# Recurrence with gated MLP on one core: level six and the state's products moved up behind the products into y

## The chip, the cores and the metric

The kernel runs on one core of a Trainium2 chip. The metric is device time in microseconds of one launch. The median before the change is 585.6 us over three runs (585.32 to 585.61). Engines are named as the profile names them: PE is TensorE's matmul, PEld its weight load, DVE is VectorE, ACT is ScalarE, POOL is GpSimd, and SP issues most of the transfers.

## The reference

All arrays are float32. The first half is a linear recurrence with a decay per channel (batch 4, 8 heads, 768 tokens, head size 48). The second half is a two-layer MLP on the 3072 tokens (384 to 2048 to 384).

```python
for t in range(S):
    kt, vt, rt, wt = k[:, :, t], v[:, :, t], r[:, :, t], w[:, :, t]
    cur = einsum('bhd,bhe->bhde', u[None] * kt, vt)
    y[:, :, t] = einsum('bhd,bhde->bhe', rt, state + cur)
    state = wt[:, :, :, None] * state + einsum('bhd,bhe->bhde', kt, vt)
x = y.transpose(0, 2, 1, 3).reshape(B * S, H * D)
h = x @ w_in
out = (h * erf(softplus(h))) @ w_out
```

## The kernel before

The work runs in 12 steps. A step takes 128 tokens of two batch items: 16 heads, as 8 columns n times two halves e of the partitions. Step s works on item pair s mod 2, so the state of a pair is handed on two steps later.

Inside a step the 128 tokens fall into two blocks of 64 (`HC`). What tokens of a block add to each other is found in levels: level L multiplies the right half of each block of 2^L tokens with the left half of it. `scale(s, L)` (L328) multiplies the decays of the halves into r and k in place, so level L must be through TensorE before its scaling, and its scaling before level L+1. `level_products` (L552) makes the small products, 64x32 or 32x32 on a quarter of the array, and `take_level` puts them into `own`: on VectorE with a mask for level five (L562), on ScalarE for level six (L569). The steps 5 to 11 are called late; there, levels one to four are made by VectorE and GpSimd instead, on rows of 16 tokens each.

A late step (`attend_late`) does this, and the order in the code is the order on each engine, since the schedule is manual:

- `from_own(before, ..., 1)` and `fence` (L593): half of the products of the step before into the accumulator `y`. Then level five, its scaling and its take.
- `from_own(before, ..., 0)` and `through_state` (L610): the other half, and the products of the state with r into `y`. ScalarE copies the result to `xT`, the input of the MLP.
- level six and `spread_blocks(s + 1, pp)` (L672), two small products that bring the decays `over_blocks` of the next step onto 64 partitions; ScalarE copies them to `few`, and two transfers (`g_rows`, `spread`) carry them back, spread over 128 partitions.
- `kT *= spread` (L718) on VectorE, `state_part` (L659) on TensorE: k times v for both blocks. `middle` (L736) is the state between the two blocks, `S_next` (L743) that after them. `faded` (L713, L739) is the state times its decay, on GpSimd.
- `prepare(s + 1)`, a generator called `following`: its pieces are GpSimd's products of decays (L402, `tot_sb`, and `over_blocks`), the terms for distances 1 to 15 between tokens (`term`, L463 and L467; 0 to 4 on VectorE, beginning at L470, 5 to 15 on GpSimd in room that the first sums set free), their sums (L453), and the way over `by_blocks` and `by_tokens` into the next `own` (L514). `kT` of the next step takes the same kind of way over `k_blocks`.

Between these stands MLP work, laid out by letters in `USUAL` and `LATE`, one string for each of the stages front, near, 0, 1, 2, 3, 4. `H` is a piece of the hidden layer of step s-1: 12 large products (L1027, counted as passes: 6 products show as 12) into a tile `m`, copied to `h` by ScalarE (L1036). `P` is a piece of the projection of step s-3: 8 products (`project_fast`, L1142) into one of two `m` tiles, with ScalarE copies (L1148, L1153, L1156) and VectorE adds (L1162 reads the first, L1167 the second). `s`, `e` and `m` are softplus (L983), erf (L987, into `y` or the second small PSUM tile) and multiply (L992) of a chunk of h. `S1` to `S4` are blends of h (L1119, L1121, L1125, L1123), `k..` copies for them (L1100), and `F` is the next piece of `following`. `w` is one of four differences of weights, made once (L1194).

`ps_m` has two buffers: the H pieces and the projection take turns in them. `ps_p` has two tiles, pp0 and pp1, one buffer each: a new tile of a name waits until the old one is read.

Of the kernel before, what the change touches and what calls it, by code (L numbers as in the profile page):

```python
# [11 lines left out]
FP32 = mybir.dt.float32  # L12
# [5 lines left out]
P = 128  # L18
# [43 lines left out]
def kernel(  # L62
# [50 lines left out]
    over_blocks = const.tile([P, C // NEAR, JP], FP32, name="over_blocks")  # L113
# [240 lines left out]
    def prepare(s):  # L354
# [61 lines left out]
        if s == DIRECT:  # L416
            yield
        else:
            half = view(tots[NEAR_LOG + 1], 1, [[2, NC], [C >> NEAR_LOG + 1, JP]])
            quarter, last = (  # L420
                view(tots[NEAR_LOG], n, [[4, NC], [C >> NEAR_LOG, JP]]) for n in (1, 3)
            )
            to = over_blocks[:].rearrange("p (h b) n -> p b h n", h=NC)
            nc.gpsimd.tensor_mul(to[:, 0], quarter, half)
            nc.gpsimd.tensor_copy(out=to[:, 1], in_=half)
            nc.gpsimd.tensor_copy(out=to[:, 2], in_=last)
            yield
# [239 lines left out]
    def spread_blocks(s, pp):  # L667


        n = D // 2  # L670
        for e in range(NE):
            nc.tensor.matmul(  # L672
                pp[:EP, e, 0:2, HC // 2 : HC // 2 + n],
                lhsT=over_blocks[rows(e)].rearrange("p b n -> p (b n)"),
                rhs=ident[rows(e), rows(e)], start=True, stop=True,
            )
        few = att.tile([EP, NE * 2, n], FP32, name="few", bufs=1)
        nc.scalar.copy(
            few[:].rearrange("p (e i) d -> p e i d", e=NE),
            pp[:EP, :, 0:2, HC // 2 : HC // 2 + n],  # L680
        )
        g_rows = dram.tile([C // NEAR, JP * NE * D], FP32, name="g_rows")
        nc.sync.dma_start(
            out=g_rows[:].rearrange("b (n d) -> (b n) d", n=JP),
            in_=few[:].rearrange("p i d -> p (i d)"),
        )
        spread[s] = att.tile([P, JP, NE, D], FP32, name="spread", bufs=1)
        nc.sync.dma_start(
            out=spread[s][:].rearrange("p n e d -> p (n e d)"),
            in_=g_rows[:, None, :].to_broadcast([C // NEAR, NEAR, JP * NE * D]),  # L690
        )

    def attend_late(s, run):
# [10 lines left out]
        take_level(own, pp, LOG - 1)  # L704
        run("front", None)
        if before:
            from_own(before, ready[before][0], 0)
            through_state(before, xTs[before])
            if s + 1 < n_steps:
                load_step(s + 1)  # L710
        following = prepare(s + 1) if s + 1 < n_steps else iter(())
        next(following, None)
        nc.gpsimd.tensor_mul(faded[0][:], S[:], ends[:, :, 0:1].to_broadcast([P, JP, D]))  # L713
        next(following, None)
        run("near", None)
        next(following, None)
        kT = kTs[s]
        nc.vector.tensor_mul(  # L718
            kT[:].rearrange("p (e n) d -> p n e d", e=NE),
            kT[:].rearrange("p (e n) d -> p n e d", e=NE), spread[s][:],  # L720
        )
        run(0, following)

        pp = products([P, NE, JP, HC], 0)
        level_products(pp, RK, LOG)
        if s + 1 < n_steps:
            spread_blocks(s + 1, pp)
        take_level(own, pp, LOG)
        scale(s, LOG)
        run(1, following)  # L730
        ps = products([P, NC, JP, HC], 0)
        ps = [[ps[:, h]] * NE for h in range(NC)]
        state_part(s, kT, ps)
        run(2, following)
        for e in range(NE):
            nc.vector.tensor_add(middle[rows(e)], faded[0][rows(e)], ps[0][e][rows(e), :, :D])  # L736
        run(3, following)
# [6 lines left out]
        run(4, following)  # L744
# [575 lines left out]
    def in_order(s, k):  # L1320
# [3 lines left out]
        for what in order[k]:  # L1324
# [15 lines left out]
            "s P", "m w", "ey P m s P P ep P", "m P P", "", "", ""  # L1340
# [72 lines left out]
    with tc.manual_schedule(  # L1413
# [77 lines left out]
        run_late(s - 1, "S Q w w w")  # L1491
# [105 lines left out]
```

## Time and profile before

| what | value |
|---|---|
| median of three runs | 585.6 us |
| the profiled execution | 586.88 us |
| its span, first to last instruction | 585.1 us |
| granted TensorE clock | 0.999 |
| PE busy | 576.4 us (99%) |
| DVE busy | 454.7 us (78%) |
| ACT busy | 355.6 us (61%) |
| POOL busy | 274.1 us (47%) |
| late steps, start of level five | 196.14, 241.46, 286.21, 330.71, 375.21, 419.71, 464.20 us |

A line of a timeline gives the start in the span, the duration, the engine, the line of the code, the operation, the tile written and the tiles read, the shapes and how many instructions were merged. In square brackets stands how long the engine was idle before, and what ended that. TensorE products in float32 show as two passes each, so 32 products count as 64. Consecutive products overlap, so the time a group takes is read from the starts, not from the durations.

### The profile page before, as it was taken

To read this page: it belongs to the slowest core of one execution; us is meant where nothing else is said; L and a number is where in the kernel's file an instruction comes from. 1 tells how busy PE (TensorE), PEld (TensorE's weight loads), DVE (VectorE), ACT (ScalarE), POOL (GpSimd) and SP (SyncE) were. 2 spreads that over 40 slices of the span, in tenths; PEclk is the share of its full clock that TensorE was granted. 3 is DMA by queue.
4 is the path that set the end of the run, shared out by engine and by line. 5 is a ranking of instruction groups with operands and counts; after the bars stand their busy time and mean duration, and the time that the engine had idled before them with its cause. 6 is when DMAs were issued, how large, how long until landed. Compare 5 with 4: busy or idle time off the path is not lost.

```text
span 585.1 us, 16663 instructions
## 1 busy us (share of the span) xinstructions
PE 576.4 (99%) x7240; PEld 495.1 (85%) x7240; DVE 454.7 (78%) x558; ACT 355.6 (61%) x478; POOL 274.1 (47%) x313
## 2 busy tenths in 40 slices
PE   8899999999999999999999999999999999999997
PEld 6588887688668758998898898898898899988997
DVE  6776886999996899799799799799799637256630
ACT  3658877644544598756766666665765771387700
POOL 4557391702398469659459459449549200000000
PEclk9999999999999999999999999999999999999999
DMA  8587571440433414334334334334331301000000
GB/s 269 177 273 281 201 235 44 183 154 10 145 95 116 117 55 156 63 116 165 74 111 169 74 108 172 75 108 136 74 108 55 74 8 36 2 0 2 28 27 29
DMA packets 54082, 63.25 MB, mean 108 GB/s; under 512 B 35160, under 2 KB 40568, under 8 KB 52984
## 3 DMA queue, kind: packets, MB, share of 16 engines
q1 hardware_dynamic: 53624, 61.98, 33.4%
q8 instruction: 57, 0.93, 0.6%
q10 hardware_dynamic: 384, 0.20, 0.1%
q14 instruction: 17, 0.14, 0.1%
HBM read 52.39 MB, written 8.69 MB: 104 GB/s over the span
## 4 chain that ended last, share of the span: by engine, by line
PE 95%; DVE 3%; issue 1%; ACT 0%; POOL 0%; DVEq 0%; POOLq 0%
PE m L1027 36%; PE m L1142 28%; PE m L1059 8%; PE pp L552 6%; PE pp L1230 4%; PE y L1230 2%; PE y L584 2%; PE pp L659 2%; PE y L610 2%; PE m L862 1%; PE pp L871 1%; PE pp L938 1%; DVE in L328 1%; DVE words L467 1%; PE pp L1142 0%
## 5 line engine op out<-in xcount | busy, mean ns | idle before, releaser
L1027 PE MATMUL m<-xT,w_in_sb 128*128 128x256 f32 x960 | 215.3, 382 | 0.1
L1027 PEld LDWEIGHTS m<-xT,w_in_sb 128*128 128x128 f32 x960 | 179.9, 190 | 26.2 <-issue 1.0
L328 DVE TENSOR_TENSOR in<-in,tot_sb 128x1024 f32<-128x1024 f32 (+1 forms) x55 | 75.3, 1369 | 16.5 <-PE pp L552 13.2
L463 POOL TENSOR_TENSOR rk<-words 128x528 f32<-128x528 f32 (+3 forms) x28 | 42.5, 1517 | 91.2 <-DVE sums L453 80.7
L1036 ACT COPY h<-m 128x512 f32<-128x512 f32 x80 | 46.4, 579 | 57.6 <-PE m L1027 57.5
L467 POOL TENSOR_TENSOR words<-words,rest 128x528 f32<-128x528 f32 (+10 forms) x77 | 78.1, 1015 | 6.0
L1059 PE MATMUL m<-w_out_sb,h 128*128 128x384 f32 x192 | 64.3, 491 | 0.0
L1059 PEld LDWEIGHTS m<-w_out_sb,h 128*128 128x128 f32 x192 | 35.7, 190 | 23.5
L1142 PE MATMUL m<-mixed,h 128*128 128x192 f32 x256 | 45.6, 331 | 0.0
L1142 PE MATMUL m<-w_out_sb,h 128*128 128x192 f32 x256 | 44.8, 329 | 0.0
L552 PEld LDWEIGHTS pp<-in 48*64 48x64 f32 (+1 forms) x2368 | 33.4, 126 | 12.0 <-issue 6.2
L1142 PEld LDWEIGHTS m<-mixed,h 128*128 128x128 f32 x256 | 41.4, 190 | 0.9
L1142 PEld LDWEIGHTS m<-w_out_sb,h 128*128 128x128 f32 x256 | 41.6, 190 | 0.3
L1142 PE MATMUL m<-w_out_sb,room 128*128 128x192 f32 x240 | 41.5, 326 | 0.0
L983 ACT ACT_TABLE_LOAD x30 | 38.5, 1283 | 2.7 <-issue 2.2
L987 ACT ACT_TABLE_LOAD x30 | 38.5, 1283 | 1.5 <-DVE room L1125 1.1
L1142 PEld LDWEIGHTS m<-w_out_sb,room 128*128 128x128 f32 x240 | 39.4, 190 | 0.0
L402 POOL TENSOR_TENSOR tot_sb<-tot_sb 128x256 f32<-128x256 f32 (+4 forms) x50 | 36.2, 724 | 3.8
L552 PE MATMUL pp<-in 48*64 48x32 f32 (+1 forms) x2368 | 37.3, 212 | 0.6 <-DVE in L328 0.5
L463 POOL TENSOR_TENSOR words<-words 128x336 f32<-128x336 f32 (+6 forms) x49 | 35.3, 720 | 3.8
L453 DVE TENSOR_REDUCE sums<-rk 128x14 f32<-128x672 f32 (+9 forms) x54 | 34.7, 701 | 0.0
L453 DVE TENSOR_REDUCE sums<-words 128x6 f32<-128x288 f32 (+8 forms) x66 | 26.9, 464 | 3.9 <-POOL words L463 3.6
(198 smaller groups left out, 951.5 us busy)
## 6 DMA issues: line engine op xcount, KB each, us to landing
in<-in_rkw SPq DMA_DIRECT2D x8, 1024.0 KB, 5.1
words<-in_moe_w_in SPq DMA_DIRECT2D x16, 384.0 KB, 5.4
words<-in_moe_w_out SPq DMA_DIRECT2D x16, 384.0 KB, 4.7
words<-in_rk_rows SPq DMA_DIRECT2D x8, 768.0 KB, 5.6
w<-in_rkw SPq DMA_DIRECT2D x11, 512.0 KB
v<-in_v SPq DMA_DIRECT2D x12, 384.0 KB, 5.6
out<-o SPq DMA_DIRECT2D x23, 192.0 KB, 2.4
in<-in_rkw SPq DMA_DIRECT2D x7, 512.0 KB, 5.7
```

What stands on the lines that cost most here:

```text
L328: nc.vector.tensor_mul(halves, halves, view(tots[level - 1], 0, [[1, n], [2, nb], [0, half]]))
L402: nc.gpsimd.tensor_mul(new, pair[:, :, 0], pair[:, :, 1])
L453: nc.vector.tensor_reduce(out=view(sums[:], n, [[near * (NEAR + 1), NEAR // near], [NEAR + 1, near - n]]), in_=terms[n], axis=mybir.AxisLi ...
L463: engine.tensor_mul(terms[n], r[:, :, n:], k[:, :, : near - n])
L467: engine.tensor_mul(k[:, :, :m], k[:, :, :m], w[:, :, n : n + m])
L552: nc.tensor.matmul(to, lhsT=rk(1, n)[rows(e), s0 : s0 + m], rhs=right, start=True, stop=True,)
L983: nc.scalar.activation(sp_room, chunks[0], AF.Softplus)
L987: nc.scalar.activation(at, sp_room, AF.Erf)
L1027: nc.tensor.matmul(ps[:, ff, :], lhsT=w_in_sb[:, g * FG + f + ff, kk * P : (kk + 1) * P], rhs=xT[:, kk, :], start=kk == 0, stop=kk == KT - 1,)
L1036: nc.scalar.copy(h[:, f : f + FT, :], ps[:])
L1059: nc.tensor.matmul(ps[j][:], lhsT=gs[g][:, f, j * C : (j + 1) * C], rhs=w_out_sb[:, g * FG + f, :], start=g + f == 0, stop=g == NG - 1 and ...
L1142: nc.tensor.matmul(to, lhsT=a[:, f], rhs=b[:, f], start=start and f == 0, stop=f == FG - 1, skip_group_check=True,)
```

## The change

In the late steps, level six and the state's products follow directly behind `through_state`. The kT multiply moves up behind the take of level five, and the stage "near" (a multiply of h) and the first `faded` move up with it. The state's products go to tile pp1 and level six to pp0. Then come the take of level six, the first piece of `following`, the middle adds, the scaling of level six, the second `faded` and the S_next adds, and only then the next two pieces of `following`, stage 0, the spread product and the stages 1 to 4. The spread product for the steps from 6 on becomes one product over all 128 partitions, with 128 columns of weights and 96 of the identity, in a tile of its own; `over_blocks` is twice as large for it, with the second half staying at one. In the last step one `w` moves from "near" to the list behind it.

```diff
-    over_blocks = const.tile([P, C // NEAR, JP], FP32, name="over_blocks")
+    over_blocks = const.tile([P, 2, C // NEAR, JP], FP32, name="over_blocks")
...
-            to = over_blocks[:].rearrange("p (h b) n -> p b h n", h=NC)
+            to = over_blocks[:, 0].rearrange("p (h b) n -> p b h n", h=NC)
...
-    def spread_blocks(s, pp):
-        n = D // 2
-        for e in range(NE):
+    def spread_blocks(s, pp=None):
+        few = att.tile([EP, NE, D], FP32, name="few", bufs=1)
+        if s > DIRECT + 1:
+            got = products([P, NE * JP * HC], 0)[:, : NE * D].rearrange("p (e d) -> p e d", e=NE)
             nc.tensor.matmul(
-                pp[:EP, e, 0:2, HC // 2 : HC // 2 + n],
-                lhsT=over_blocks[rows(e)].rearrange("p b n -> p (b n)"),
-                rhs=ident[rows(e), rows(e)], start=True, stop=True,
+                got, lhsT=over_blocks[:].rearrange("p i b n -> p (i b n)"),
+                rhs=ident[:].rearrange("p (e m) -> p e m", e=NE)[:, :, :D],
+                start=True, stop=True,
             )
-        few = att.tile([EP, NE * 2, n], FP32, name="few", bufs=1)
-        nc.scalar.copy(
-            few[:].rearrange("p (e i) d -> p e i d", e=NE),
-            pp[:EP, :, 0:2, HC // 2 : HC // 2 + n],
-        )
+            nc.scalar.copy(few[:], got[:EP])
+        else:
...
         take_level(own, pp, LOG - 1)
+        kT = kTs[s]
+        nc.vector.tensor_mul(
+            kT[:].rearrange("p (e n) d -> p n e d", e=NE),
+            kT[:].rearrange("p (e n) d -> p n e d", e=NE), spread[s][:],
+        )
+        nc.gpsimd.tensor_mul(faded[0][:], S[:], ends[:, :, 0:1].to_broadcast([P, JP, D]))
         run("front", None)
+        run("near", None)
         if before:
             from_own(before, ready[before][0], 0)
             through_state(before, xTs[before])
             if s + 1 < n_steps:
                 load_step(s + 1)
+        pp = products([P, NE, JP, HC], 0)
+        level_products(pp, RK, LOG)
+        ps = products([P, NC, JP, HC], 1)
+        ps = [[ps[:, h]] * NE for h in range(NC)]
+        state_part(s, kT, ps)
+        take_level(own, pp, LOG)
         following = prepare(s + 1) if s + 1 < n_steps else iter(())
         next(following, None)
-        nc.gpsimd.tensor_mul(faded[0][:], S[:], ends[:, :, 0:1].to_broadcast([P, JP, D]))
-        next(following, None)
-        run("near", None)
-        next(following, None)
-        kT = kTs[s]
-        nc.vector.tensor_mul(
-            kT[:].rearrange("p (e n) d -> p n e d", e=NE),
-            kT[:].rearrange("p (e n) d -> p n e d", e=NE), spread[s][:],
-        )
-        run(0, following)
-
-        pp = products([P, NE, JP, HC], 0)
-        level_products(pp, RK, LOG)
-        if s + 1 < n_steps:
-            spread_blocks(s + 1, pp)
-        take_level(own, pp, LOG)
-        scale(s, LOG)
-        run(1, following)
-        ps = products([P, NC, JP, HC], 0)
-        ps = [[ps[:, h]] * NE for h in range(NC)]
-        state_part(s, kT, ps)
-        run(2, following)
         for e in range(NE):
             nc.vector.tensor_add(middle[rows(e)], faded[0][rows(e)], ps[0][e][rows(e), :, :D])
-        run(3, following)
+        scale(s, LOG)
         if s < n_steps - SPC:
             nc.gpsimd.tensor_mul(
                 faded[1][:], middle[:], ends[:, :, 1:2].to_broadcast([P, JP, D])
             )
             for e in range(NE):
                 nc.vector.tensor_add(S_next[rows(e)], faded[1][rows(e)], ps[1][e][rows(e), :, :D])
-        run(4, following)
+        next(following, None)
+        next(following, None)
+        run(0, following)
+        if s + 1 < n_steps:
+            spread_blocks(s + 1)
+        for n in range(1, 5):
+            run(n, following)
...
         n_steps - 1: (
-            "s P", "m w", "ey P m s P P ep P", "m P P", "", "", ""
+            "s P", "m", "ey P m s P P ep P", "m P P", "", "", ""
         ),
...
-        run_late(s - 1, "S Q w w w")
+        run_late(s - 1, "S Q w w w w")
```

The branch left out keeps the two small products into level six's tile for the spread product of step 5, which step 4 still issues in its old place. On the queues, SP's transfers keep their order. On each other engine the instructions are the same but for the spread product, in the new order described.

More of the change, by code (lines that the diff above doesn't have):

```diff
@@ L665, in state_part @@
                     )
-    def spread_blocks(s, pp):
-        n = D // 2
-        for e in range(NE):
+    def spread_blocks(s, pp=None):
+        few = att.tile([EP, NE, D], FP32, name="few", bufs=1)
+        if s > DIRECT + 1:
+            got = products([P, NE * JP * HC], 0)[:, : NE * D].rearrange("p (e d) -> p e d", e=NE)
             nc.tensor.matmul(
-                pp[:EP, e, 0:2, HC // 2 : HC // 2 + n],
-                lhsT=over_blocks[rows(e)].rearrange("p b n -> p (b n)"),
-                rhs=ident[rows(e), rows(e)], start=True, stop=True,
-            )
-        few = att.tile([EP, NE * 2, n], FP32, name="few", bufs=1)
-        nc.scalar.copy(
-            few[:].rearrange("p (e i) d -> p e i d", e=NE),
-            pp[:EP, :, 0:2, HC // 2 : HC // 2 + n],
-        )
+                got, lhsT=over_blocks[:].rearrange("p i b n -> p (i b n)"),
+                rhs=ident[:].rearrange("p (e m) -> p e m", e=NE)[:, :, :D],
+                start=True, stop=True,
+            )
+            nc.scalar.copy(few[:], got[:EP])
+        else:
+            n = D // 2
+            got = pp[:EP, :, 0:2, HC // 2 : HC // 2 + n]
+            for e in range(NE):
+                nc.tensor.matmul(
+                    got[:, e], lhsT=over_blocks[rows(e), 0].rearrange("p b n -> p (b n)"),
+                    rhs=ident[rows(e), rows(e)], start=True, stop=True,
+                )
+            nc.scalar.copy(few[:].rearrange("p e (i d) -> p e i d", i=2), got)
         g_rows = dram.tile([C // NEAR, JP * NE * D], FP32, name="g_rows")
@@ L684, in spread_blocks @@
             out=g_rows[:].rearrange("b (n d) -> (b n) d", n=JP),
-            in_=few[:].rearrange("p i d -> p (i d)"),
+            in_=few[:].rearrange("p e d -> p (e d)"),
         )
@@ L704, in attend_late @@
         take_level(own, pp, LOG - 1)
+        kT = kTs[s]
+        nc.vector.tensor_mul(
+            kT[:].rearrange("p (e n) d -> p n e d", e=NE),
+            kT[:].rearrange("p (e n) d -> p n e d", e=NE), spread[s][:],
+        )
+        nc.gpsimd.tensor_mul(faded[0][:], S[:], ends[:, :, 0:1].to_broadcast([P, JP, D]))
         run("front", None)
+        run("near", None)
         if before:
```

## The prediction

> **What bounds the kernel now.** I read the page first (busy time, chain of waits), then the timelines of the engines, stretch by stretch, in the late steps. A late step s is named by its level-five products (L552, 48x64): steps 5, 6, 7, 8, 9, 10 and 11 begin at 196.14, 241.46, 286.21, 330.71, 375.21, 419.71 and 464.20 us, so a step takes 44.75 us once and 44.50 otherwise. Step 9 is my model, and all offsets below count from 375.21.
>
> The page, busy time and chain by engine:
>
> ```profile
> PE 576.4 (99%) x7240; PEld 495.1 (85%) x7240; DVE 454.7 (78%) x558; ACT 355.6 (61%) x478; POOL 274.1 (47%) x313
> ...
> PE 95%; DVE 3%; issue 1%; ACT 0%; POOL 0%; DVEq 0%; POOLq 0%
> ```
>
> TensorE has almost no idle time: only work taken off it can be won, and any wait put on it is lost. Its timeline in step 9 (start, duration, group; each product shows as two passes):
>
> ```profile
> 375.21 1.09 PE L552 MATMUL pp<-in 48*64 48x32 f32 x64
> ...
> 379.96 0.63 PE L610 MATMUL y<-in,middle 48*48 48x64 f32 x32
> 380.51 2.87 PE L1142 MATMUL m<-mixed,h 128*128 128x192 f32 x16
> 383.22 2.76 PE L1142 MATMUL m<-w_out_sb,room 128*128 128x192 f32 x16
> ...
> 388.42 2.76 PE L1142 MATMUL m<-w_out_sb,room 128*128 128x192 f32 x16
> 391.11 0.76 PE L552 MATMUL pp<-in 48*32 48x32 f32 x64
> 391.80 0.32 PE L672 MATMUL pp<-ident,over_blocks 48*64 48x48 f32 x4
> 392.05 2.87 PE L1142 MATMUL m<-mixed,h 128*128 128x192 f32 x16
> ...
> 397.44 0.94 PE L659 MATMUL pp<-v,kT 64*48 64x48 f32 x64
> 398.31 20.99 PE L1027 MATMUL m<-xT,w_in_sb 128*128 128x256 f32 x96
> ```
>
> VectorE, ScalarE and GpSimd in the same step:
>
> ```profile
> 378.11 0.96 DVE L470 TENSOR_TENSOR words<-words,u_row 128x768 f32<-128x768 f32 x1
> ...
> 391.73 1.72 DVE L718 TENSOR_TENSOR kT<-kT,spread 128x768 f32<-128x768 f32 x1
> ...
> 396.24 0.54 DVE L1162 TENSOR_TENSOR o<-o,m 128x384 f32<-128x384 f32 x1
> ...
> 402.23 1.21 DVE L1119 TENSOR_TENSOR room<-h,y 128x1024 f32<-128x1024 f32 x1
> ...
> 417.98 1.22 DVE L514 TENSOR_TENSOR own<-block_sb,by_tokens 128x1024 f32<-128x1024 f32 x1 [2.15 <-DMA by_tokens<-by_blocks]
> ```
>
> ```profile
> 403.47 1.02 ACT L1100 COPY y<-h 128x1024 f32<-128x1024 f32 x1 [1.68 <-DVE room L1119]
> 404.42 0.58 ACT L1036 COPY h<-m 128x512 f32<-128x512 f32 x1
> ```
>
> ```profile
> 387.92 1.31 POOL L463 TENSOR_TENSOR rk<-words 128x528 f32<-128x528 f32 x1 [14.56 <-DVE sums L453]
> ```
>
> What to see: TensorE's next work hangs on VectorE by short slacks. The hidden products H (398.31) reuse the m tile that L1162 reads; it ends at 396.78, 1.53 before. L1119 releases ScalarE's copy at 403.47, behind which the second copy h<-m stands; it ends at 405.00, and the fourth H piece needs it at 398.31 + 3 x 2.615 = 406.16. VectorE has about 4.5 us a step to spare (40.00 busy in the 44.50 of step 9), and spends it waiting.
>
> **What TensorE saves.** A run of 16 passes 128x192 takes 2.60 (383.22 to 385.82), 2.71 after small products, 2.69 before them (388.42 to 391.11); the last group of the state's products takes 0.55 before a large one and 0.45 before a small one (379.51 to 379.96). Now two places where small products interrupt go: 0.20 at the ends of small groups, 0.11 and 0.18 at the large ones. The spread product leaves the small group (0.25 there, 0.10 of it the end of the group) and stands alone with 2 passes 128x96: at least 0.16 by the pitch of the 256- and 192-column rows (218 and 163 ns, 0.85 ns a column), at most 0.38 by the 190 ns weight load of 128x128; I take 0.30. Net about 0.33 a step, 2 us in all.
>
> **What moves on VectorE.** Before, the terms of the next step (L470 on) follow level five at offset 2.90. Now the kT multiply, the h multiply of "near", both middle adds, the scaling of level six and both S_next adds stand ahead of them, and the middle adds wait for the state's products. Offsets: scaling and take of level five 1.16 and 2.30, kT 2.90, h multiply 3.78 to 4.99. TensorE: one P until 3.81, own and state products until 5.20, level six 0.69, state's products 0.87, end 6.76. So the products do not wait in step 9. Middle starts 0.2 later (as at 487.22) at 6.96, 2 adds 1.14; scaling 0.60 to 8.70; GpSimd's faded (0.84, 0.14 after the adds) ends at 9.05; S_next 1.15, end 10.23. The terms start at 10.23 instead of 2.90.
>
> From there in the queue's order: terms 7.70, sums 4.79 (386.94 to 391.73), two h multiplies 1.13 each: L1162 runs from 24.98 to 25.52, before it ended at 21.57. TensorE, without waits, has its P's done at 6.76 + 10.51 (2.71 and three of 2.60) + 0.30 + 5.20 = 22.8. So **H starts at 25.6, after a wait of 2.8**. Next L1119: 24.98 + 0.46 + 1.65 + 0.46 + 3.42 = 30.97 (before 27.02), so the second h copy ends 3.95 later, at 33.74. H's fourth piece, due at 25.6 + 7.85 = 33.45, waits 0.3; the fifth and sixth wait 0.1 to 0.2 each for the copies behind. H ends at 47.4, the next level five comes at 47.85. **A steady step costs 47.85 instead of 44.50.** ScalarE's level-six copies (1.16) now stand before its first erf; the erf still ends near offset 9.5, long before the multiply at 22.7 needs it: nothing. Its "few" copy (0.23) comes later in the queue and opens g_rows and spread, which land some 25 us before the kT multiply that reads them, also at its new place: nothing, and 0.23 if ScalarE had none to spare. The larger over_blocks is set once, at 3.0; a memset of 384 columns took 0.42, so at most that, and nothing where GpSimd waits later.
>
> **GpSimd and the transfers.** GpSimd's terms start 0.98 into the first sum: 10.23 + 7.70 + 0.98 = 18.91 (before 12.71). Their chain to the last L463 took 23.22 (387.92 to 411.14); some products are slow beside VectorE (2.03 for 1.31). The kT multiply and level six's scaling leave it: 1.0 less, by the slow products beside them (1.80 for 1.22, 1.56 for 1.11). End 41.1. Then by SP's rows k_blocks +0.38, by_blocks +0.45, by_tokens +2.26 to 2.82, landing for L514 +3.19: 47.4 to 48.0. Level five's scaling then starts at the next offset 1.16 or up to 0.4 late; the state's products have 0.9 to spare (5.89 against 4.99). kT, issued 0.47 after by_tokens and 4.7 in flight, lands at 49.4 to 50.0, wanted at 50.75. Just covered: if the cover goes, each us late costs one us a step. SP keeps its order; no transfer passes another. The `w` that moves to the end (1.23) had idle time at 468.23 and now precedes the token differences, which end at 498.96, 3.3 before 502.27: nothing.
>
> kT takes 0.96 where GpSimd has no work (at 469.37) and 1.72 beside it; by the order GpSimd is idle there, so I take 0.96, and 0.76 more a step as the other bound.
>
> The Trainium skill, "SBUF — State Buffer", section "SBUF: two separate sides", says that VectorE and GpSimd share a port pair that is locked for a whole instruction, the loser blocking fully. By that rule the kT multiply, now on the path to the state's products, could wait out a whole GpSimd product (2.03) rather than lose 0.76; the spare 0.9 would not hold and a step would be about 1.1 longer, some 4 us in all. The rows show no such full block for this multiply, so I do not add it.
>
> **Step 5** has no products of an earlier late step and no P between level five and six. Level six waits for the take of level five (198.75 + 0.61): 199.45; the state's products for kT (199.36 + 0.96): 200.35, end 201.2. Before, P's ran from 197.16; with the 0.69 + 0.87 done early, H is due at 201.2 + 13.0 + 0.3 + 7.95 = 222.45 (the P's as at 197.16 and 211.19) instead of 219.99. VectorE's h multiply waits for ScalarE's erf (204.49), so the terms start at 208.95 instead of 199.36. L1119 comes 20.8 later (7.70, 4.79, three h multiplies 3.4, scalings 1.65 to 2.1 and 3.05), at 229.75 (before 224.49); the second h copy ends at 232.5, the fourth H piece waits 2.1 for it, and step 6 begins at 246.6 instead of 241.46: +5.1. GpSimd's weight subtraction (3.45) then pushes its totals beside the front of step 6; 0 to 1.5 late, I take 0.8.
>
> **Sum.** 5.1 + 0.8 + 3.1 (step 6, 47.85 - 44.75) + 3 x 3.35 (7 to 9) + 1.8 (step 10, which has no S_next and so gains 1.53 of the 3.35) - 0.35 (step 11, no next terms) = 20.5. The profiled execution took 586.88, span 585.1 and 1.78 around it; its span becomes 605.6. The three runs' median is 585.6, 1.28 below it; the sum lands on the median as 606.1.
>
> **Rivals.**
> 1. VectorE and ScalarE stay covered; only TensorE's own terms remain: +2.5 in step 5, -2 elsewhere, 586. It needs L1162 2.4 us earlier than worked out. Against: it is in order behind the wait for the state's products.
> 2. Faster: merging frees more than the pitches show. From 0.6 us a step on (7 steps, 4.2 against 2.5 and the 1.2 of 0.2%) it decides, if 1 holds too; at 0.8 the time is 582.5. Against: pitches 2.60, 2.69, 2.71.
> 3. Only the m tile is waited for, ScalarE's copies keep up: steps of 25.6 + 20.92 + 0.48 = 47.0, step 5 +2.9: 2.9 + 2.25 + 7.5 + 1.0 - 0.35 = 13.3, 599.
> 4. GpSimd and transfers become the bound: chain 23.22, transfers at 2.82 and 3.4, level five's scaling and kT at their slow 1.75 and 1.65 pitch: steps of 49.9: 5.1 + 1.5 + 5.15 + 16.2 + 3.9 - 0.35 = 31.5, 617.
>
> **Numbers.** Main case 0.69, rival 1 0.05, rival 2 0.03, rival 3 0.11, rival 4 0.12. The range 598 to 615 holds the main case, nearly all of 3 and the lower part of 4. A measurement tells about 0.2% (1.2 us) from no change: faster 0.03, same 0.04, slower 0.93.
>
> **What would show it.** Right: idle TensorE before the first L1030 of a step, released by VectorE's L1165; waits inside H for L1039 copies; L470 some 10 us after level five; steps near 47.9; idle TensorE before level six in step 5. Wrong: steps at 44.2 (rivals 1, 2); waits before the state's products for kT or own (4). My largest risk is the start of the terms: each us there is a us in every step.

## The result, and the profile after

The changed kernel takes 619.75 us (median of five runs, 617.28 to 620.46), the kernel before 585.35 us (585.25 to 585.61). The ratio is 1.058, with a 95% interval of 1.0559 to 1.0602: 34.4 us slower, where 20.5 was predicted. The direction and the place were right; the time lies 4.75 us above the range.

The profiled execution took 619.82 us, its span is 617.9 (before 585.1), and the mean granted clock of TensorE fell from 0.999 to 0.986. In the changed file the lines from 673 on have moved: L1162 is now L1165, L1027 is L1030, L1036 is L1039, L1119 is L1122, L1142 is L1145, L718 is L712, and the adds L736 and L743 are L733 and L740. The fades L713 and L739 are L716 and L736.

From the page, busy time by engine and the shares of the chain that ended last:

```profile
PE 586.7 (95%) x7228; PEld 501.4 (81%) x7228; DVE 457.0 (74%) x558; ACT 356.1 (58%) x478; POOL 271.8 (44%) x313
...
PE 49%; DVE 21%; POOL 16%; issue 10%; ACT 2%; DMA 1%; SPq 1%; POOLq 0%; DVEq 0%; ACTq 0%
```

Before, TensorE was 95% of the chain. Now half of the chain runs over VectorE, GpSimd and "issue", time in which an engine waited for nothing that the profile shows. TensorE is also busy 10 us longer with the same products but for the spread: they run slower somewhere.

Level five of the steps 5 to 11 now begins at 194.94, 245.96, 295.36, 345.43, 397.70, 447.38 and 493.98 us. The steps take 51.02, 49.40, 50.07, 52.27, 49.68 and 46.60 us (before 45.32, 44.75, then 44.50 and 44.49), and 123.92 follow from step 11 on (before 120.90). Step 8, the slowest, on TensorE:

```profile
345.43 1.09 PE L552 MATMUL pp<-in 48*64 48x32 f32 x64
...
350.17 0.63 PE L610 MATMUL y<-in,middle 48*48 48x64 f32 x32
350.73 0.76 PE L552 MATMUL pp<-in 48*32 48x32 f32 x64
351.42 0.51 PE L659 MATMUL pp<-v,kT 64*48 64x48 f32 x25
353.33 0.66 PE L659 MATMUL pp<-v,kT 64*48 64x48 f32 x39 [1.40 <-issue]
353.92 2.87 PE L1145 MATMUL m<-mixed,h 128*128 128x192 f32 x16
...
364.42 0.36 PE L673 MATMUL pp<-ident,over_blocks 128*128 128x96 f32 x2
...
367.25 2.76 PE L1145 MATMUL m<-w_out_sb,h 128*128 128x192 f32 x16
373.30 23.98 PE L1030 MATMUL m<-xT,w_in_sb 128*128 128x256 f32 x96 [3.29 <-DVE o L1165]
397.21 0.66 PE L584 MATMUL y<-own,v 64*48 64x64 f32 x32
```

Three things are to be seen. The long group of small products is interrupted inside the products of the state, 1.40 us, and no engine is named for it. The hidden products H wait 3.29 us for VectorE's L1165, where the prediction had put a wait of 2.8. And they then take 23.91 us (373.30 to 397.21) where the same 96 passes took 20.92 before.

The same step on VectorE, and GpSimd's second fade between the two pairs of adds:

```profile
348.34 0.94 DVE L712 TENSOR_TENSOR kT<-kT,spread 128x768 f32<-128x768 f32 x1
...
354.12 1.12 DVE L733 TENSOR_TENSOR middle<-faded,pp 48x384 f32<-48x384 f32 x2 [3.71 <-PE pp L659]
...
356.69 1.11 DVE L740 TENSOR_TENSOR s<-faded,pp 48x384 f32<-48x384 f32 x2 [0.73 <-POOL faded L736]
357.83 0.96 DVE L470 TENSOR_TENSOR words<-words,u_row 128x768 f32<-128x768 f32 x1
...
372.70 0.55 DVE L1165 TENSOR_TENSOR o<-o,m 128x384 f32<-128x384 f32 x1
```

```profile
355.32 1.34 POOL L736 TENSOR_TENSOR faded<-middle,tot_sb 128x384 f32<-128x384 f32 x1 [11.19 <-DVE middle L733]
```

VectorE stands idle for 3.71 us behind the h multiply, because the adds of `middle` wait for the last product of the state. The terms start 12.40 us after level five (2.90 before), and everything behind them is that late.

What TensorE waited for in the whole execution:

```profile
PE m L1030 <- DVE o L1165: 13.4, 5, 3.3
PE pp L659 <- issue: 3.5, 3, 1.4
PE m L1030 <- ACT h L1039: 2.4, 4, 1.0
PE pp L552 <- DVE own L562: 2.4, 1, 2.4
...
PE pp L552 <- issue: 1.3, 1, 1.3
PE m L1145 <- issue: 1.0, 1, 1.0
```

The three lines on "issue" are the pauses, 5.8 us. The granted clock in the H of step 7 and of step 8, each after a wait of 3.29 us, and in the slow part of the latter alone (columns: window, its length, busy time and count of PE, PEld, DVE, ACT and POOL, granted clock, DMA share, GB/s):

```profile
323.10:345.00 21.90, 21.76 (x100) 17.97 (x103) 17.32 (x22) 15.49 (x18) 19.30 (x28) 1.00 0.44 136
373.30:397.30 24.00, 24.00 (x100) 20.31 (x104) 18.36 (x22) 15.53 (x18) 19.28 (x28) 0.87 0.47 131
372.57:379.40 6.83, 6.10 (x14) 4.83 (x15) 6.79 (x7) 2.54 (x3) 6.59 (x4) 0.50 0.55 172
```

After the same wait the clock once stays, and once it falls to 0.87 on the mean of the next 24 us: to 0.50 for 6.83 us, and 1.00 behind that. H took 21.83 in step 7 and 23.91 in step 8, so the low clock is 2.1 of the 3 us. The other 0.9 stands in step 7 too, at full clock. The prediction had 21.8 for H, with waits for ScalarE's copies in it.

### The profile page after: what moved, and what is told of

Read it like the earlier page. It is cut to its first block, busy times and chain, and to the rows that moved or that the text cites. A ratio compares the mean times of both kernels' runs of the same rounds, so it can differ in the third digit from the quotient of the medians.

```text
span 617.9 us, 16625 instructions
## 1 busy us (share of the span) xinstructions
PE 586.7 (95%) x7228; PEld 501.4 (81%) x7228; DVE 457.0 (74%) x558; ACT 356.1 (58%) x478; POOL 271.8 (44%) x313
## 4 chain that ended last, share of the span: by engine, by line
PE 49%; DVE 21%; POOL 16%; issue 10%; ACT 2%; DMA 1%; SPq 1%; POOLq 0%; DVEq 0%; ACTq 0%
PE m L1030 16%; PE m L1145 13%; POOL words L467 6%; DVE in L328 4%; PE pp L552 4%; PE pp L1233 4%; DVE words L467 4%; PE m L1062 3%; DVE sums L453 3%; DVE rk L463 3%; POOL tot_sb L402 3%; POOL words L463 2%; PE y L1233 2%; POOL rk L463 2%; PE y L584 1%
## 5 line engine op out<-in xcount | busy, mean ns | idle before, releaser
L1030 PE MATMUL m<-xT,w_in_sb 128*128 128x256 f32 x960 | 222.6, 389 | 16.0 <-DVE o L1165 13.4
L1030 PEld LDWEIGHTS m<-xT,w_in_sb 128*128 128x128 f32 x960 | 182.3, 193 | 48.5 <-DVE o L1165 14.8
L328 DVE TENSOR_TENSOR in<-in,tot_sb 128x1024 f32<-128x1024 f32 (+1 forms) x55 | 79.9, 1452 | 6.0 <-PE pp L552 4.4
L467 POOL TENSOR_TENSOR words<-words,rest 128x528 f32<-128x528 f32 (+10 forms) x77 | 79.4, 1031 | 6.0
L1039 ACT COPY h<-m 128x512 f32<-128x512 f32 x80 | 46.3, 579 | 57.0 <-PE m L1030 56.6
L463 POOL TENSOR_TENSOR rk<-words 128x528 f32<-128x528 f32 (+3 forms) x28 | 40.3, 1440 | 78.4 <-DVE sums L453 68.0
L1145 PE MATMUL m<-mixed,h 128*128 128x192 f32 x256 | 46.9, 338 | 1.0 <-issue 1.0
L1145 PE MATMUL m<-w_out_sb,h 128*128 128x192 f32 x256 | 44.8, 329 | 0.0
L1145 PEld LDWEIGHTS m<-mixed,h 128*128 128x128 f32 x256 | 43.1, 196 | 1.6 <-issue 1.2
L1145 PEld LDWEIGHTS m<-w_out_sb,h 128*128 128x128 f32 x256 | 41.6, 190 | 0.3
L1145 PE MATMUL m<-w_out_sb,room 128*128 128x192 f32 x240 | 41.5, 326 | 0.0
L1103 ACT COPY y<-h 128x1024 f32<-128x1024 f32 x12 | 12.2, 1017 | 50.4 <-DVE h L995 37.2
L1145 PEld LDWEIGHTS m<-w_out_sb,room 128*128 128x128 f32 x240 | 39.4, 190 | 0.0
L402 POOL TENSOR_TENSOR tot_sb<-tot_sb 128x256 f32<-128x256 f32 (+4 forms) x50 | 37.7, 755 | 3.8
L453 DVE TENSOR_REDUCE sums<-rk 128x14 f32<-128x672 f32 (+9 forms) x54 | 34.7, 701 | 0.0
```

The lines of the kernel that those rows point to most:

```text
L328: nc.vector.tensor_mul(halves, halves, view(tots[level - 1], 0, [[1, n], [2, nb], [0, half]]))
L402: nc.gpsimd.tensor_mul(new, pair[:, :, 0], pair[:, :, 1])
L453: nc.vector.tensor_reduce(out=view(sums[:], n, [[near * (NEAR + 1), NEAR // near], [NEAR + 1, near - n]]), in_=terms[n], axis=mybir.AxisLi ...
L463: engine.tensor_mul(terms[n], r[:, :, n:], k[:, :, : near - n])
L467: engine.tensor_mul(k[:, :, :m], k[:, :, :m], w[:, :, n : n + m])
L1030: nc.tensor.matmul(ps[:, ff, :], lhsT=w_in_sb[:, g * FG + f + ff, kk * P : (kk + 1) * P], rhs=xT[:, kk, :], start=kk == 0, stop=kk == KT - 1,)
```

## The experiments

The theory after the result has three parts. (1) VectorE's late terms hold TensorE. (2) TensorE's long group of small products costs by itself, through pauses at borders of its instruction stream. (3) Waits and pauses pull the granted clock down. The main rival: the group, not VectorE's order, makes the loss. Medians, ratios to the kernel before on the same chip, and what each kernel is (the code cuts below are shortened):

| run | what | us | ratio |
|---|---|---|---|
| e10 | before, with level six and own products moved, two groups of 128 passes | 583.99 | 0.9991 [0.9978, 1.0003] |
| e7 | before, with level six alone moved | 585.76 | 1.0018 [0.9998, 1.0039] |
| e9 | group of the change split by one P, VectorE's old order | 586.65 | 1.0036 [1.0022, 1.0049] |
| e8 | group of the change, VectorE's old order | 596.42 | 1.0212 [1.0179, 1.0245] |
| e2 | e1, and the group split by one P | 603.01 | 1.0319 [1.0272, 1.0366] |
| e1 | the change, terms put first on VectorE | 603.17 | 1.0319 [1.0293, 1.0344] |
| e6 | before, VectorE held up by 3.9 us a step | 609.75 | 1.0426 [1.0395, 1.0456] |
| e5 | the change, step 5 in the old order | 611.41 | 1.046 [1.044, 1.0481] |
| e4 | the change, large products ahead of H | 611.87 | 1.0463 [1.044, 1.0486] |
| after | the change | 619.75 | 1.058 [1.0559, 1.0602] |

e3 shifts the instruction stream and is read by its trace alone. e3, e4 and e6 do extra work whose result is not used or is written again unchanged. Each file has its own line numbers from some 470 on; the names of the tiles tell the instructions.

### e1: the terms first

```diff
         following = prepare(s + 1) if s + 1 < n_steps else iter(())
         next(following, None)
+        next(following, None)
         for e in range(NE):
             nc.vector.tensor_add(middle[rows(e)], ...)
...
-        next(following, None)
         next(following, None)
         run(0, following)
```

> The changed kernel, but VectorE makes the terms of the next step (L470 to L467) ahead of the middle adds, which are what waits for the state's products; TensorE's group of small products stays whole. Theory A (the terms start late because they stand behind that wait, and the m tile is set free late): L470 about 5 us after level five instead of 12.4, the first L1030 waits for VectorE's add by under 0.5 us instead of 2.2 to 3.3, steps 6 to 9 near 46.0 us instead of 49.4 to 52.3, about 601 us in all. Theory B (the long group itself costs the time, by pauses of TensorE's own and a lower clock): 616 to 620 us as before this edit.

603.17 us, 16.6 less than the change. The terms start 4.90 us after level five, no wait is shown at the start of an H any more, and the steps 6 to 9 take 46.42 to 46.44. Step 5 takes 54.06, with a pause of 2.03 in its group and a low clock around it (0.56 from 198.1 to 205.0). Step 8 on TensorE, and VectorE's add ahead of it:

```profile
363.71 7.98 PE L1030 MATMUL m<-xT,w_in_sb 128*128 128x256 f32 x36
371.85 13.73 PE L1030 MATMUL m<-xT,w_in_sb 128*128 128x256 f32 x60 [0.16 <-ACT h L1039]
```

```profile
363.05 0.55 DVE L1165 TENSOR_TENSOR o<-o,m 128x384 f32<-128x384 f32 x1
```

Part (1) holds: the place of one piece of `following` on VectorE is worth half of the loss. In step 8, H starts 0.11 after L1165 ends, and the four steps are equal though their pauses are not (0.85 to 1.60), so VectorE still seems to set them: the adds of `middle` and of the next state and the scaling of level six stand ahead of L1165.

### e2: the terms first, and the group split

```diff
             if s + 1 < n_steps:
                 load_step(s + 1)
+            run_late(s, "P")
         pp = products([P, NE, JP, HC], 0)
         level_products(pp, RK, LOG)
```

(with e1's edit, and one P fewer in stage 0)

> As e1_terms_first, but one P of stage 0 stands between the products of the state into y and level six, so that the group of small products is cut into 96 and 128 passes. If the pauses of 0.9 to 1.4 us that TensorE shows inside the state's products come from the length of the group, they vanish and step 11 loses about 2.9 us (pause and low clock behind it): about 598 us; the steps 6 to 9 hardly move, since VectorE's add sets their H. If the pauses come from something else, they stay, and the time is that of e1_terms_first plus 0.3 us a step.

603.01 us instead of the 598 expected: nothing won. The pauses are gone from step 6 on, but the steps stay at 46.42 to 46.45:

```profile
225.00 23.62 PE L1031 MATMUL m<-xT,w_in_sb 128*128 128x256 f32 x96 [4.71 <-ACT o L1072]
...
365.99 8.04 PE L1031 MATMUL m<-xT,w_in_sb 128*128 128x256 f32 x36 [0.33 <-DVE o L1166]
```

With the pauses away, H waits 0.33 for VectorE: they had been in the shade of its order. Step 5 shows the same. Its H starts 30.93 us after level five, 0.05 after ScalarE's copy L1072 ends; in e1 it started at 30.60, 0.49 after that copy, without a wait shown. So the pause of 2.03 and the slow products of e1 had been hidden there too, nearly all of them, and taking them away left TensorE to wait 4.71.

### e3: the instruction stream shifted

Small passes counted from the start of the group (own products 32, through the state 64, level six 64, state 64), the pauses of the change stand after 228, 207, 185, 164 and 153 passes in the steps 6, 7, 8, 9 and 11; in step 10 it would be 142, and there is none. They move by 21.5 a step, 32 passes being left out in step 10, as a border every 128 passes would: the timeline shows 530 passes a step, 18 more than 4 x 128, and the other 3.5 would be 7 instructions a step that are no products or loads (not shown). From the page, the queue that carries instructions:

```profile
q8 instruction: 57, 0.93, 0.6%
```

57 packets for TensorE's 14,456 instructions (products and loads) are 254 each; 128 passes with their loads are 256. That this queue is TensorE's is read from this agreement and from the shift below. To test the border, 32 tiny products (64 passes) were put at the start of the program:

```diff
+        tiny = ps_m.tile([P, NC, P], FP32, name="m")
+        for _ in range(32):
+            nc.tensor.matmul(
+                tiny[:EP, 0, :16], lhsT=ident[:EP, :EP], rhs=ident[:EP, :16], ...)
```

> The changed kernel with 32 tiny products (64 passes, 128 matmul and weight-load instructions) added at the very start, where TensorE waits for data anyway. If the pauses are the fetch of TensorE's instructions at block borders, every pause moves 64 passes earlier in its group: in the steps 6, 7, 8, 9 and 11 from the passes 228, 207, 185, 164 and 153 behind the start of the group to 164, 143, 121, 100 and 89. If a pause is a wait for other engines or comes from the length of the group, it stays where it was. Time within 2 us of the changed kernel either way.

Each border must come 64 passes earlier: step 6 at 164 instead of 228; step 9 at 100, and the next one at 228. Of the five pauses expected only that of step 6 is there, at its place. At 143, 121, 100 and 89, in the steps 7, 8, 9 and 11, nothing pauses; step 9 pauses at its next border instead.

```profile
269.05 0.92 PE L659 MATMUL pp<-v,kT 64*48 64x48 f32 x60 [1.05 <-issue]
...
418.73 2.22 PE L1145 MATMUL m<-mixed,h 128*128 128x192 f32 x12 [0.77 <-issue]
```

Step 6 pauses with 60 of 64 products left (160 + 4 = 164), step 9 after 4 passes of the P (224 + 4 = 228). The time of 627.83 us was expected within 2 us of the change and is 8 above it: the clock was 0.50 from 10.8 to 34.7 us, behind the tiny products, and step 5 comes 16 us later. From there on the run takes 7 us less than the change.

### e4: large products ahead of H

```diff
+            if n == 2 and DIRECT + 1 < s < n_steps - 1:
+                fill = products([P, NE * JP * HC], 0)[:, : 2 * P].rearrange("p (i n) -> p i n", i=2)
+                for _ in range(6 if s < n_steps - SPC else 2):
+                    nc.tensor.matmul(
+                        fill, lhsT=ident[:], rhs=ident[:, None, :].to_broadcast([P, 2, P]), ...)
```

> The changed kernel with dummy 128x256 products (6 in the steps 6 to 9, 2 in step 10) in front of the first L1030, where TensorE waits 2.2 to 3.3 us for VectorE. If the low clock that two of the four H runs show (22.6 and 23.9 us for 96 passes, granted clock 0.92 and 0.87, against 21.8) follows from that idle time, all H runs take 21.8 and the clock up to step 10 is 1.00: 3 us less, about 616.5 us. If the clock has another cause, two of the H runs stay long and the time stays at 619.7.

611.87 us, 7.9 less than the change although TensorE has more to do. The H of the steps 7 to 10 take 21.9 us, the waits at their start shrink to 0.46 to 0.72, and the pauses stand 12 passes earlier in step 7, 24 in step 8, and are gone in step 9 (164 - 36 = 128), as the border theory has it:

```profile
351.27 0.93 PE L659 MATMUL pp<-v,kT 64*48 64x48 f32 x63 [1.02 <-issue]
371.52 21.91 PE L1037 MATMUL m<-xT,w_in_sb 128*128 128x256 f32 x96 [0.70 <-DVE o L1172]
```

The expected 616.5 us counted the clock alone, and the trace tells the rest apart. Step 8 is 2.4 us shorter and step 6 is 0.8 shorter, mostly since their H run at a clock of 1.00 (21.84 and 21.54 us instead of 23.91 and 22.61). Step 9 is 1.1 shorter and what follows from step 11 on 3.0, for their pauses are gone. So the idle time at this place also costs clock afterwards, some 3 us in all.

### e5: step 5 in the old order

For step 5 `attend_late` is the old one, for the others the new one.

```diff
+        if s == DIRECT + 1:
+            ...  # the body of the kernel before
+            return
```

> The changed kernel with step 5 alone put back into the old order (level six and the products of the state at their old places, VectorE's order as before); steps 6 to 11 keep the new one. Level five of step 5 to level five of step 6 took 45.3 us before and 51.0 after. Theory (each step pays for its own group, by itself): step 5 goes back to 45.3, the other steps stay at 49.4 to 52.3 (their pauses move by two small products only), so 619.8 - 5.7 = about 614 us, 612 to 616. Rival (the delay is carried on: the rest of the late stage is set by something that does not depend on step 5, and gives the time back or loses more): steps 6 to 11 change by over 1 us each and the time is outside 610 to 617.

611.41 us, 0.6 under the expected range's lower end. In the trace step 5 takes 45.25 (before 45.32), and the steps 6 to 10 together 247.13 against 248.02. Single steps differ by up to 2.3, since the low clock falls into other H's (the steps 6, 7 and 9 instead of 6 and 8). On the whole each step pays for itself.

### e6: VectorE held up in the kernel before

```diff
+        for _ in range(4 if s > DIRECT + 1 else 0):
+            nc.vector.tensor_mul(terms[0], k, u_times)
```

> The kernel before, in which VectorE's first multiply of the terms (0.88 us in the trace) is done five times instead of once in the late steps: the same values are written again, and the first term of the next step comes about 3.5 us later on VectorE; TensorE's order is untouched, and no group of small products is made longer. Theory A (the late terms by themselves hold TensorE, through the near block and the copies): the half products of the late steps wait about 2 us for VectorE, ScalarE's copies of the first parts follow late, and a step of 44.5 takes 46.5 to 48; six such steps give 598 to 608 us. Rival B (it takes the long group of small products and its pauses; VectorE has slack of more than 3.5 us there): 585.0 to 588, no wait of TensorE for VectorE before the half products.

609.75 us. TensorE's order and its groups are those of before; only VectorE's first term is made five times (0.95 and 3.94 us). Step 7 on VectorE and on TensorE:

```profile
298.25 3.94 DVE L472 TENSOR_TENSOR words<-words,u_row 128x768 f32<-128x768 f32 x4
...
319.35 0.54 DVE L1164 TENSOR_TENSOR o<-o,m 128x384 f32<-128x384 f32 x1
```

```profile
319.95 22.67 PE L1029 MATMUL m<-xT,w_in_sb 128*128 128x256 f32 x96 [2.24 <-DVE o L1164]
```

The prediction had read a slack of 1.53 us between this add and H. A delay of 3.94 less 1.53 is 2.41: H waits 2.24, and 0.2 goes into the group before it. The step costs 48.67 instead of 44.50, 4.17 more and not 2.41, for H takes 22.60 (319.95 to 342.55) instead of 20.92, at a granted clock of 0.92:

```profile
321.29:324.70 3.41, 3.41 (x10) 2.72 (x9) 3.31 (x4) 0.65 (x2) 3.25 (x3) 0.50 0.50 144
```

In the steps 6 and 10 the clock stayed at 1.00 after the same wait, and H still took 22.06, with two waits of 0.16 and 0.20 for ScalarE's copies of h in it. So 1.1 of the 1.7 come without a low clock, through copies that stand behind the late work of VectorE. The low clock adds 0.5, for an H that runs at it shows no wait for copies. This is part (3) without any long group, but a small part of the price.

### e7: level six alone

```diff
             through_state(before, xTs[before])
             if s + 1 < n_steps:
                 load_step(s + 1)
+            pp = products([P, NE, JP, HC], 0)
+            level_products(pp, RK, LOG)
+            take_level(own, pp, LOG)
```

(the old place keeps the spread product, now one; the state's products stay where they were)

> The kernel before with one part of the change alone: in the late steps level six follows on the products of the state into y, the spread is one small product in the place of the old level six, and the products of the state, VectorE's and GpSimd's orders stay. The group of small products has 160 passes instead of 96. Theory A (VectorE's order costs, the merge by itself saves the pair of changes of shape, about 0.15 to 0.3 us in each of six steps): 583.5 to 585 us. Rival B (a group of that length pauses at the borders of the instruction stream by 0.8 to 1.4 us in two or three of the six steps, and more than eats the gain): 586 to 589.

585.76 us, ratio 1.0018 [0.9998, 1.0039]: no difference that can be told. The steps 7 and 8 take 44.27 and 44.28, so one group less with the single spread product saves 0.22. The group of 160 passes pauses twice, after 161 and after 149 passes, for 0.61 and 0.35 us:

```profile
379.65 2.71 PE L1153 MATMUL m<-mixed,h 128*128 128x192 f32 x15 [0.61 <-issue]
...
468.35 0.31 PE L552 MATMUL pp<-in 48*32 48x32 f32 x11 [0.35 <-issue]
```

### e8: the whole group, VectorE in the old order

```diff
+        kT = kTs[s]
+        if before:
+            nc.vector.tensor_mul(kT..., spread[s][:])
         run("front", None)
         if before:
+            run("near", None)
             from_own(before, ready[before][0], 0)
             through_state(before, xTs[before])
+            pp = products([P, NE, JP, HC], 1)
+            level_products(pp, RK, LOG)
+            ps = products([P, NC, JP, HC], 0)
+            state_part(s, kT, ps)
+            take_level(own, pp, LOG)
+            run_late(s, "P")
+            spread_blocks(s + 1)
```

(the terms, the adds, level six's scaling and the second fade stay at their old places; step 5 is the old one)

> TensorE's whole new group (products of the state into y, level six, products of the state) in steps 6 to 11, with the old order of the rest: the terms of the next step come first on VectorE, the middle, the scales, the second fade and the next state stay at their old places; step 5 in the old order; of VectorE's work only the multiply of kT and the last step's near block come ahead of the terms. Theory A (VectorE's order was what cost): no wait of TensorE on VectorE before the half products, the merge saves about 2 us in all, pauses inside the group take 0.8 to 1.4 in three or four steps, sum 585 to 591. Rival B (the group costs by itself, through the late start of the first passes and ScalarE's copies behind them): as with the terms put first in the new order, 46.4 per step, 595 to 600.

596.42 us: theory A's range is missed, and rival B's is met, though by pauses and not by what B named, as e9 shows. No H waits for VectorE at its start, as A said, but the group costs 12 us and not 1 to 6. The steps 5 to 10 take 46.22, 45.33, 45.86, 47.97, 46.00 and 44.89, and 123.99 follow; the pauses are 0.47, 1.06, 1.62, 1.21 and, in step 11, 1.30, and behind two of them a P runs at a low clock. Step 8:

```profile
339.77 0.98 PE L659 MATMUL pp<-v,kT 64*48 64x48 f32 x39 [1.62 <-issue]
340.68 4.15 PE L1166 MATMUL m<-mixed,h 128*128 128x192 f32 x16
```

A P of 16 passes takes 2.71 behind small products; this one takes 3.99 (340.68 to 344.67), and that of step 11 takes 4.35.

### e9: the same, with the group split

```diff
                 load_step(s + 1)
+            run_late(s, "P")
             pp = products([P, NE, JP, HC], 1)
```

(and one P fewer in stage 0)

> As the run with TensorE's whole group and VectorE's old order, but one P of 2.8 us stands between the products of the state into y and level six, so that the group of 224 small passes becomes one of 96 and one of 128. Theory (the group's own price is the pauses at the borders of the instruction stream, which only come after some 150 small passes, and the low granted clock behind them): no pause of TensorE inside or behind a group from step 6 on, no P of over 3 us, steps of 44.3 to 44.7, the rest behind step 11 back at 121; 585 us, 583.5 to 588. Rival (the early place of level six and of the state's products costs by itself, through ScalarE's copies or the buffers): steps stay at 45.3 or more without a pause, 590 to 597.

586.65 us, 9.8 under e8. The edit only moves one P between the products of the state and level six. Of the 11.2 us between the two profiled spans, 8.7 lie in the steps from 6 on; the five pauses of e8 (5.7) and its two slow P's (2.9) make 8.6. There is no pause from step 5 on, no P at a low clock, and the steps 6 to 10 take 44.73 to 44.80, a little over the 44.3 to 44.7 expected. Step 8:

```profile
335.58 0.76 PE L552 MATMUL pp<-in 48*32 48x32 f32 x64
336.27 0.94 PE L659 MATMUL pp<-v,kT 64*48 64x48 f32 x64
337.13 2.87 PE L1167 MATMUL m<-w_out_sb,room 128*128 128x192 f32 x16
...
342.66 2.76 PE L1167 MATMUL m<-w_out_sb,room 128*128 128x192 f32 x16
345.61 2.87 PE L1167 MATMUL m<-mixed,h 128*128 128x192 f32 x16 [0.19 <-ACT o L1181]
```

This shows part (2). The same small products pause as one run of 224 passes and not as 96 and 128. What is left of the 44.75 against 44.50 fits the wait for ScalarE's copy L1181, in whose queue level six's copies now come earlier; no run takes that wait away. It is given as 0.19, but the pitches tell 0.46: 342.66 to 345.61 is 2.95 instead of 2.60, and the P behind it takes 2.71.

### e10: two groups of 128 passes

```diff
-        run("front", None)
         if before:
             from_own(before, ready[before][0], 0)
+        run("front", None)
+        if before:
             through_state(before, xTs[before])
```

(on top of e7)

> The kernel before with level six behind the products of the state into y, as in the run of level six alone, and in addition the second half of the own products ahead of the P in front of them, behind level five: 128 small passes, one P, 128 small passes. Theory: the step keeps the 0.22 us that the one group less saved (44.28 instead of 44.50) and the pauses of 0.35 and 0.61 are gone; 6 x 0.22 = 1.3 us under the kernel before, a ratio of 0.9978. Rival (the second own products must wait for VectorE's copy that separates them from the first, which now lies only one level of products ahead): a wait of 0.3 to 1 us in each step ahead of them, the same time as before or up to 4 us more.

583.99 us, ratio 0.9991 [0.9978, 1.0003]. The steps 7 to 10 take 44.29, 44.29, 44.29 and 44.28, with no pause and no wait for the second own products:

```profile
327.77 1.09 PE L552 MATMUL pp<-in 48*64 48x32 f32 x64
328.68 0.64 PE L584 MATMUL y<-own,v 64*48 64x64 f32 x32
329.25 2.87 PE L1154 MATMUL m<-w_out_sb,h 128*128 128x192 f32 x16
...
333.09 0.76 PE L552 MATMUL pp<-in 48*32 48x32 f32 x64
```

The gain of 0.21 a step is plain in the trace; as a time, some 1 us over the late steps, it is at the bound of what can be told: the interval includes no change. None of the arrangements here beats the kernel before by more than that.

## Why the prediction was right or wrong

**The mechanism was right.** VectorE's terms behind the adds, L1165 late, H waiting for it: in the trace of the change, and by e1 and e6 in both directions. From the terms to L1165 14.87 us were measured in step 8 (14.75 predicted). Step 10 was predicted at 46.29 and took 46.60. Step 5 was predicted at 51.22 and took 51.02, in part by luck: its H began 27.39 us after level five and not 26.31, with the clock at 0.50 for 3.41 us behind the wait ahead of level six, its waits for copies were 1.28 and not 2.1, and the 0.8 for GpSimd's totals do not show. Rivals 1, 2 and 3 fell: their steps were 44 to 47. Rival 4's time (617) came closest, but not its mechanism: from step 6 on no product waits for kT or for own, and the scaling of level five behind L514 still waits for TensorE (0.44 us in step 8).

**"A steady step costs 47.85" is the step that failed.** The steps 6 to 9 took 49.40, 50.07, 52.27 and 49.68, together 10.0 us more than 4 x 47.85. Three of its terms were wrong; the pauses and the clock had been put at nothing:

- *"state's products 0.87, end 6.76".* The terms were to start at 10.23 and started at 10.84, 12.28, 12.40 and 11.89; H began 6.9 us later in all. The pauses of the steps 7, 8 and 9 (1.28, 1.40, 0.86) stand inside the state's products, for which the adds wait. By the starts the group lost 4.3 with them, more than the 3.5 shown as idle. The trace of the kernel before had such pauses, at its beginning, 128 passes apart, and the prediction put the inside of the group at no wait:

```profile
23.81 0.43 PE L659 MATMUL pp<-v,kT 64*48 64x48 f32 x11 [0.88 <-issue]
...
29.40 0.56 PE L552 MATMUL pp<-rk 48*64 48x64 f32 x18 [1.26 <-issue]
```

- *The second fade, 0.84.* GpSimd's L736 took 1.34, which puts the next adds 0.45 later in each step, 1.8 in all. VectorE's scaling of level six runs beside it; where it does not (the kernel before, e7, e8, e9), the fade takes 0.83 to 0.84. "My largest risk is the start of the terms" named the place, and its size was missed.
- *H takes 20.92 plus some waits for copies.* It took 3.1 us more in all than predicted, nearly all of it in the steps 6 and 8, at a granted clock of 0.92 and 0.87. The prediction had no term for the clock. In the steps 7 and 9, at 1.00, H took 21.8, as predicted.

**"TensorE's products do not wait in step 9" and "merging saves 0.33 a step".** No work of another engine held the group, as predicted, but the group held itself. The merge of half the groups measured 0.22 (e7, e10). Of the whole merge, step 10, which has no pause, shows TensorE done with its P's at 22.9 us after level five; 22.8 was predicted. So this term was right where no pause fell into the group, though by two small misses that cancel: the products into y took 0.10 more, for the 0.45 "before a small one" was 0.55 ahead of level six, and the spread product took 0.19 instead of 0.30.

**"-0.35 for step 11" was +3.0.** The group of step 11 pauses after 153 passes, and the first P behind it runs at a low clock, 4.37 us (502.27 to 506.64) instead of 2.71:

```profile
501.23 0.26 PE L552 MATMUL pp<-in 48*32 48x32 f32 x7 [1.25 <-issue]
...
502.27 4.53 PE L1145 MATMUL m<-mixed,h 128*128 128x192 f32 x16
```

The balance of the span: step 5 -0.2, steps 6 to 9 +10.0, step 10 +0.3, from step 11 on +3.4, and the beginning 1.2 earlier than before. The two pauses at the beginning of the kernel before, 2.1 us, are not in the profiled execution of the change, and the runs above reach step 5 at 192.7 to 196.5 though their edits hardly touch what comes first (e3 apart). That is the 12.3 us between the predicted span of 605.6 and 617.9.

**The kT multiply, and the blocking between VectorE and GpSimd.** It took 0.94 us in step 8, as assumed (0.96). The rule that the prediction weighed, of a full block for a whole GpSimd product, would have put up to 2.03 us there; it is not put to the test, because GpSimd is idle at that time. Nor do the rows speak against a block, as the prediction held: in the kernel before, the kT multiply began at 391.73 beside a GpSimd product that ran until 392.64, 0.91 more, and lost 0.76. The second fade began 0.64 before the end of VectorE's scaling and lost 0.5. Both fit a wait for most of what the other still had to do.

**Where the 34 us come from**, as a ladder of runs. TensorE's new order with the group split: +0.36% (e9), 2 us. The group in one piece: +1.8% (e8), 10 us; by the traces 8.6 of them are pauses and slow P's behind them. Step 5 in the new order, and the adds, the scaling and the fade ahead of L1165: +1.1% (e1), 6 us; by the traces it lies in step 5, 54.06 against 46.22, while the steps 6 to 10 of e1 and e8 sum up to the same 230, once by VectorE's order and once by pauses. The terms behind the adds: +2.6% (the change), 15 us. A ladder in another order would split the sum differently, since pauses hide in waits, as e1 against e2 shows.

**What stays open.** That the borders are those of instruction blocks rests on the spacing of 128 passes, which e3 and e4 confirm, on the number of the packets, and on their times (below); no run changed the size of an instruction block, and why a packet starts when it does is not shown. The clock after a wait was not predictable from these runs: the same 3.29 us gave 1.00 in two steps and 0.87 in one.

## What to carry to other kernels

Before an instruction is moved ahead on one engine, find what stands behind its consumers on the next engine's queue: here the adds that wait for the state's products pushed a chain of 15 us in front of TensorE, and one call's place was worth 16.6 us of 34.4. A run of small products is cheap only while it is short: in the steps from 6 on, 96 and 128 passes ran through, and some 150 and more could pause for 0.35 to 1.6 us, so a large piece of work between them is worth more than the 0.2 us that a merge saves. And on an engine that is 99% busy a delay can cost more than itself: 2.41 us cost 4.17 in e6, for the copies of ScalarE came later too, and in some steps the clock fell.

## What was not expected of the hardware

- **TensorE pauses at borders of its instruction stream.** From step 6 on for 0.35 to 1.6 us, at positions 128 passes apart, and only where about 150 or more small passes had run without a large product between them. That is not the whole rule: the longest pause, 2.03 in step 5 of e1, stands 122 passes behind a wait of 2.40 us, and the second one at the beginning of the kernel before stands 14 small passes behind 6 large ones. The transfer of a block of instructions starts ahead of each pause in the late steps of the change. The view of the transfers, cut to 350.6 to 350.8 us of the change, has the start of one:

```profile
q8 instruction: 1, 0.02, 38.0%
```

  The pause begins at 351.93 and ends at 353.33, some 2.6 us after that start; in the steps 6, 7, 9 and 11 it is 2.2 to 2.3 us from the start of the packet to the first product after the pause. A block of 128 small passes lasts 1.75 us at 13.6 ns a pass (160 passes in the 2.18 us from 349.24 to 351.42), shorter than that. The Trainium skill, "Runtime: NRT & Kernel Launch", section "Instruction fetch mechanics", says that an engine's instructions come in blocks of 256 and that crossing a border is mostly hidden. The 256 agree with the 128 passes; "mostly hidden" holds in the late steps of the kernel before, which have no pause, and not here.
- **The granted clock falls after waits of 2 to 3 us, but not always.** 0.92 after 2.17 and 2.24, 0.87 and 1.00 after 3.29; 0.61 in the 4.4 us after a pause of 1.25 in step 11. Cut finer, each of these means is 0.50 for 3.41 us, or for 6.83 in step 8, and 1.00 for the rest. In e4, where large products shortened the waits to 0.72 at most, it was 1.00 in the H of the steps 6 to 10.
- **A wait shown as 0.19 us costs 0.46** between runs of large products: the runs ahead of it and behind it take 2.95 and 2.71 instead of 2.60 (e9).
